# Sixty-four row scatters declared disjoint, and the expert weights moved in the POOL queue

## The chip, the cores and the metric

One core of one Trainium2 chip runs the whole program in one launch. The metric is the time of one execution in microseconds, taken on the device. Engines named here: PE (matrix multiply), DVE and ACT (elementwise), POOL (GpSimd, which also issues the indirect DMAs and the weight loads), SP (issues the plain DMAs).

## The reference

Linear attention with decay, then a mixture of experts with one expert per token.

- Attention: q, k, v are (4 batches, 8 heads, 768 positions, 64). Per head, with decay lam, each position gets the masked, decayed sum over its own block plus what a running 64x64 state `kv_state` of the blocks before it gives; the state is decayed and updated block by block. The result, heads side by side, is x of (3072 tokens, 512).
- Router: cosine logits of x against 8 expert embeddings, divided by tau; each token goes to its largest logit, with that softmax value as its gate.
- Experts: `out[mask] = gate * (relu(x[mask] @ w1[e]) @ w2[e])`, w1 of 512x1024 and w2 of 1024x512 for each of 8 experts, in float32 in memory.

## The kernel before, in words

The order of the instructions on every engine is the order in which they are written (a manual schedule); semaphores are put in by the framework from the tiles and DRAM tensors that instructions read and write.

**Attention** is a loop of 24 rounds of 128 tokens (6 rounds for each of 4 batches), software-pipelined: iteration i loads q, k, v of round i+3 (`load_round`, SP, a ring of 6 buffers each), transposes round i+2 on PE, makes the decayed keys `ks` of round i+2 on POOL (L242), does the output matmuls of round i, scales the state on POOL (`pool_kvt`, L295), and writes it with DVE (`ev_kv`, L307), which needs that POOL result. The first round of a batch has no state and is shorter. Iterations 0 to 7 also write zero rows into the scratch tensor (`zrow`, L470).

**Routing** goes by five groups of 6, 6, 6, 4 and 2 rounds. Once a group is done, DVE finds each token's expert and its row in the scratch `xs_dram` (one region of 3072 rows for each expert), and `scatter` (L428) sends each round's 128 rows (fp16 x, token number, gate) there with one indirect DMA issued by POOL: 24 in all. The list `todo` says at which iteration each comes; the scatters of the last two groups come after the loop's other work, the two of group 4 ahead of the four of group 3. The slot numbers `si` live in 2 buffers, used by groups in turn.

**Weights** come in 64 loads of a quarter matrix (`load_w`, L211 and L213), cast from float32 to fp16 by the DMA, issued by POOL: one in each iteration from i = 2 to 25, which brings experts 0 to 2, then eight behind each expert's scatters. `wpool` has 4 buffers for each of w1 and w2.

**Experts.** SP reads each expert's first 512 rows back (`load_xe`; expert 0 in four pieces), PE transposes them, then `pe_L1` and `pe_L2`. For each of 4 row blocks DVE scales the result into one of 6 `y_sb` buffers (L565) and POOL scatters the 128 rows to `out` (L567): 32 in all. Rows that hold no token carry an index out of bounds and are skipped. The read of expert e+4 reuses the buffer whose index column the last scatter of expert e reads. `pstart`, an iota on POOL (L516), stands between attention's last POOL work and the first of these scatters; DVE needs it (L584) before it scales the first result.

A block for experts with over 512 tokens follows the count; in this case's runs its loop bodies leave no instruction in the trace.

Of the kernel before, what the change touches and what calls it, by code (L numbers as in the profile page):

```python
# [9 lines left out]

# [11 lines left out]
def kernel(  # L22
# [19 lines left out]
    R = B * NBLK  # L42
    E, DM = moe_expert_emb.shape
# [4 lines left out]
    G = CAP // P  # L48
# [6 lines left out]
    groups = [list(range(0, 6)), list(range(6, 12)), list(range(12, 18)),  # L55
              list(range(18, 22)), list(range(22, 24))]
# [4 lines left out]

    const = ctx.enter_context(tc.tile_pool(name="const", bufs=1))
    dram = ctx.enter_context(tc.tile_pool(name="dram", bufs=1, space=bass.MemoryType.DRAM))
    wpool = ctx.enter_context(tc.tile_pool(name="wpool", bufs=4))
    xgp = ctx.enter_context(tc.tile_pool(name="xgp", bufs=3))
    rsm = ctx.enter_context(tc.tile_pool(name="rsm", bufs=2))

    xs_dram = dram.tile([E * ROWS, DM2], I32, name="xs_dram")

    w1_r = moe_w1.rearrange("e (c p) f -> e p c f", p=P)  # L70
    w2_r = moe_w2.rearrange("e (c p) d -> e p c d", p=P)
# [16 lines left out]
    def load_round(i):  # L88
        b, blk = divmod(i, NBLK)
        for src, store, nm in ((q, qn, "qn"), (k, kn, "kn"), (v, vn, "vn")):  # L90
            t = ring.tile([P, H, D], FP32, name=nm, tag=nm)
            nc.sync.dma_start(t, src[b, :, ds(blk * P, P), :].rearrange("h p d -> p h d"))
            store[i] = t
# [104 lines left out]
    wpos = [0]  # L198

    def load_w(n):  # L200
        for _ in range(n):
            if wpos[0] >= len(wq):
                return
            e, which, c = wq[wpos[0]]
            wpos[0] += 1
            if (e, 1) not in w_tiles:
                w_tiles[(e, 1)] = wpool.tile([P, DC, F], FP16, name="w1_sb", tag="w1")
                w_tiles[(e, 2)] = wpool.tile([P, FC, DM], FP16, name="w2_sb", tag="w2")
            t = w_tiles[(e, which)]
            if which == 1:  # L210
                nc.gpsimd.dma_start(t[:, c : c + 1, :], w1_r[e][:, c : c + 1, :])  # L211
            else:
                nc.gpsimd.dma_start(t[:, 2 * c : 2 * c + 2, :], w2_r[e][:, 2 * c : 2 * c + 2, :])  # L213

    def valid(i):
        return 0 <= i < R
# [15 lines left out]
    def ev_T(i):  # L232
        t = wk.tile([P, HP, P], FP32, name="qT", tag="qT", bufs=3)
        nc.vector.tensor_tensor(t, bank.pop(("q", i)), lamq, op=ALU.mult)
        qT[i] = t
        t = wk.tile([P, HP, P], FP32, name="kT", tag="kT")
        nc.scalar.copy(t, bank.pop(("k", i)))  # L237
        kT[i] = t
# [188 lines left out]

    def scatter(gi, j):  # L428
        nc.gpsimd.indirect_dma_start(  # L429
            out=xs_dram[:],  # L430
            out_offset=bass.IndirectOffsetOnAxis(ap=slot_i[gi][:, j : j + 1], axis=0),
            in_=xg[gi][:, j, :],
            in_offset=None,
        )
# [31 lines left out]
    for i in range(-2, R + 2):  # L466
        if i >= 0 and valid(i + LA):
            load_round(i + LA)
        if 0 <= i < E:
            nc.sync.dma_start(xs_dram[ds(i * ROWS, CAP), :].rearrange("(g p) d -> p g d", p=P),  # L470
                              zrow)
        if valid(i + 2):
            pe_T(i + 2)
            ev_T(i + 2)
            pool_ks(i + 2)
        if valid(i - 1):
            pe_X(i - 1)
            ev_X(i - 1)
        if valid(i - 2):
            pe_z(i - 2)  # L480
            ev_z(i - 2)
        run(i, "pe")
        if valid(i):
            pe_O(i)
            if i % NBLK < NBLK - 1:
                pe_kv(i)
                if i % NBLK > 0:
                    pool_kvt(i)
                ev_kv(i)
            ev_O(i)  # L490
        if valid(i - 1):
            pe_zT(i - 1)
            ev_zT(i - 1)
        run(i, "dve")
        if valid(i + 1):
            pe_ST(i + 1)
            ev_ST(i + 1)
        run(i, "pe2")
        run(i, "dve2")
        run(i, "pool")  # L500
        run(i, "pool2")
        if i >= 2:
            load_w(1)
    for key in sorted(todo):
        for fn, a in todo[key]:
            fn(*a)
    attn_ctx.close()


# [8 lines left out]
    with (  # L518
        tc.tile_pool(name="moe_x", bufs=4) as moe_x,
        tc.tile_pool(name="moe_sb", bufs=2) as moe_sb,  # L520
        tc.tile_pool(name="moe_y", bufs=6) as moe_y,
        tc.tile_pool(name="ps_mx", bufs=2, space=bass.MemoryType.PSUM) as ps_mx,
        tc.tile_pool(name="ps_h", bufs=3, space=bass.MemoryType.PSUM) as ps_h,
        tc.tile_pool(name="ps_y", bufs=3, space=bass.MemoryType.PSUM) as ps_y,
    ):
        xe, xTe, hT, idx = {}, {}, {}, {}

        def load_xe(e, split=1):
            t = moe_x.tile([P, G, DM2], I32, name="x_e", tag="x_e")
            src = xs_dram[ds(e * ROWS, CAP), :].rearrange("(g p) d -> p g d", p=P)  # L530
            for s in range(split):
                w = G // split
                nc.sync.dma_start(t[:, s * w : (s + 1) * w, :], src[:, s * w : (s + 1) * w, :])
            xe[e] = t

        def pe_xT(e):
            t = moe_sb.tile([P, DC, G, P], FP16, name="xTe", tag="xTe")
            for g in range(G):
                xtr = ps_mx.tile([P, DC, P], FP16, name="xtr", tag="xtr")
                for c in range(DC):  # L540
                    nc.tensor.transpose(xtr[:, c, :], xe[e][:, g, 0:DW].bitcast(FP16)[:, ds(P * c, P)], ident16)  # L541
                nc.scalar.copy(t[:, :, g, :], xtr)  # L542
            xTe[e] = t

        def pe_L1(e):
            t = moe_sb.tile([P, FC, CAP], FP16, name="hT", tag="hT")
            w = w_tiles[(e, 1)]
            for fc in range(FC):
                h_ps = ps_h.tile([P, CAP], FP32, name="h_ps", tag="h")
                for c in range(DC):  # L550
                    nc.tensor.matmul(h_ps, w[:, c, ds(P * fc, P)],  # L551
                                     xTe[e][:, c].rearrange("p g t -> p (g t)"),
                                     start=(c == 0), stop=(c == DC - 1))
                nc.scalar.activation(t[:, fc, :], h_ps, AF.Relu)  # L554
            hT[e] = t

        def pe_L2(e):
            w = w_tiles[(e, 2)]
            for g in range(G):
                y_ps = ps_y.tile([P, DM], FP32, name="y_ps", tag="y")  # L560
                for fc in range(FC):
                    nc.tensor.matmul(y_ps, hT[e][:, fc, ds(P * g, P)], w[:, fc, :],  # L562
                                     start=(fc == 0), stop=(fc == FC - 1))
                y = moe_y.tile([P, DM], FP32, name="y_sb", tag="y_sb")
                nc.vector.tensor_scalar(y, y_ps, xe[e][:, g, DW + 1 : DW + 2].bitcast(FP32),  # L565
                                        None, op0=ALU.mult)
                nc.gpsimd.indirect_dma_start(  # L567
                    out=out[:],
                    out_offset=bass.IndirectOffsetOnAxis(ap=xe[e][:, g, DW : DW + 1], axis=0),
                    in_=y[:],  # L570
                    in_offset=None,
                    bounds_check=N - 1,
                    oob_is_err=False,
                )

        load_xe(0, split=4)
        load_xe(1, split=2)
        load_xe(2)
        cnt_ps = ps_y.tile([P, DM], FP32, name="cnt_ps", tag="y")
        nc.tensor.matmul(cnt_ps[:, 0:E], ones16, ohcum, start=True, stop=True)  # L580
        nc.vector.tensor_scalar(last, cnt_ps[:, 0:E], -1.0, None, op0=ALU.add)
        nc.vector.tensor_reduce(mx, cnt_ps[:, 0:E], axis=AXL.X, op=ALU.max)

        nc.vector.tensor_tensor(  # L584
            below, cnt_ps[:, 0:E].unsqueeze(2).to_broadcast([P, E, R]),
            pstart.unsqueeze(1).to_broadcast([P, E, R]), op=ALU.is_gt)
        nc.vector.tensor_reduce(ntile_f, below, axis=AXL.X, op=ALU.add)
        nc.vector.tensor_scalar(ntile, ntile_f, float(G), None, op0=ALU.max)
        pe_xT(0)
        for e in range(E):  # L590
            pe_L1(e)
            if e + 1 < E:
                pe_xT(e + 1)
            if e + 3 < E:
                load_xe(e + 3)
            pe_L2(e)
            load_w(8)
# [5 lines left out]
    with tc.If(mreg > CAP, preferred_fallthrough_block=False):  # L603
        with (
# [5 lines left out]
            for e in range(E):  # L610
# [7 lines left out]
                with tc.For_i(G, end):  # L618
# [8 lines left out]
                        out=xo[:], out_offset=None, in_=xs_dram[:],  # L627
# [15 lines left out]
                    for fc in range(FC):  # L643
# [6 lines left out]
                        out=out[:],  # L650
# [37 lines left out]
```

## Time and profile before

| | |
|---|---|
| median of 3 runs | 392.25 us (389.97 to 394.6) |
| profiled execution | 393.91 us, of which the span from first to last instruction is 392.1 us |
[...]
| busy, of the span | PE 69%, PEld 47%, DVE 29%, ACT 31%, POOL 39% |
| DMA | 54.10 MB, mean 138 GB/s |
| weight loads | 64 of 256 KB, median 6.2 us from issue to landing |
| scatters to `xs_dram` | 24, 2.5 / 3.0 / 5.1 us to landing (min, median, max) |
| scatters to `out` | 32, 2.1 / 2.7 / 10.9 us to landing |
| DVE's scaling of one result (L565) | 751 ns, 32 of them |

Busy time is an average over an attention stage (to about 175 us), a handover (to 206 us), an expert stage (to 357 us) and a tail in which PE does nothing (to 392 us). No engine is near the full span, so the time is read from the waits of each stage. POOL's share counts the issue of its DMAs, not the time in which its queue stands behind a semaphore.

### The profile page before, as it was taken

To read this page: it belongs to the slowest core of one execution; us is meant where nothing else is said; L and a number is where in the kernel's file an instruction comes from. 1 tells how busy PE (TensorE), PEld (TensorE's weight loads), DVE (VectorE), ACT (ScalarE), POOL (GpSimd) and SP (SyncE) were. 2 spreads that over 40 slices of the span, in tenths; PEclk is the share of its full clock that TensorE was granted. 3 is DMA by queue.
4 is the path that set the end of the run, shared out by engine and by line. 5 is a ranking of instruction groups with operands and counts; after the bars stand their busy time and mean duration, and the time that the engine had idled before them with its cause. 6 is when DMAs were issued, how large, how long until landed. Compare 5 with 4: busy or idle time off the path is not lost. (4 is left out here: it accounts for less than half of the span.)

```text
span 392.1 us, 6263 instructions
## 1 busy us (share of the span) xinstructions
PE 269.1 (69%) x2426; PEld 184.6 (47%) x2426; DVE 114.8 (29%) x305; ACT 120.8 (31%) x257; POOL 152.4 (39%) x204
## 2 busy tenths in 40 slices
PE   0999897899069978930029999999979588492000
PEld 0899785899069967820014444444424134140000
DVE  2556446453157545641000302202101102012000
ACT  5244352344105442420014263362515042130000
POOL 2545162533474576263410252271532704322220
PEclk9999999899669998975557999999989979698555
DMA  9999999999969934243343139277393682921110
GB/s 164 238 251 242 242 239 216 198 213 206 228 120 184 176 72 70 41 94 67 67 129 117 43 77 214 91 145 157 88 211 103 126 178 65 183 96 38 55 75 2
DMA packets 100615, 54.10 MB, mean 138 GB/s; under 512 B 77782, under 2 KB 94166, under 8 KB 100576
## 3 DMA queue, kind: packets, MB, share of 16 engines
q0 software_dynamic: 17024, 26.25, 33.7%
q1 hardware_dynamic: 83552, 27.35, 31.7%
q8 instruction: 21, 0.34, 0.4%
q14 instruction: 18, 0.15, 0.1%
HBM read 56.68 MB, written 15.79 MB: 185 GB/s over the span
## 5 line engine op out<-in xcount | busy, mean ns | idle before, releaser
L567 POOL DMA_INDIRECT out_dram<-y_sb,x_e x32 | 32.0, 1001 | 125.9 <-issue 73.8
L551 PE MATMUL h_ps<-xTe,w_sb 128*128 128x512 f16 x256 | 65.5, 414 | 15.2 <-DMA w_sb<-in_moe_w_dram 14.4
L554 ACT ACTIVATE hT<-h_ps 128x512 f16<-128x512 f32 x64 | 38.2, 597 | 90.1 <-PE h_ps L551 90.1
L565 DVE TENSOR_SCALAR y_sb<-y_ps,x_e 128x512 f32<-128x512 f32 x32 | 24.0, 751 | 141.2 <-PE y_ps L562 70.1
L562 PE MATMUL y_ps<-w_sb,hT 128*128 128x512 f16 x256 | 56.7, 379 | 1.7 <-DVE y_sb L565 1.7
L551 PEld LDWEIGHTS <-w_sb 128*128 128x128 f16 x256 | 26.5, 105 | 53.2 <-DMA w_sb<-in_moe_w_dram 18.4
L429 POOL DMA_INDIRECT xs_dram<-xg,si x24 | 24.5, 1019 | 48.7 <-DMA xs_dram<-xg,si 35.3
L242 POOL TENSOR_TENSOR ks<-kn,kdec 128x512 f32<-128x512 f32 x24 | 25.0, 1046 | 38.5 <-DMA kn<-in_k_dram 21.2
L562 PEld LDWEIGHTS <-hT 128*128 128x128 f16 x256 | 24.7, 98 | 30.5 <-issue 2.0
L259 DVE TENSOR_TENSOR stm<-s_ps,mask 128x512 f32<-128x512 f32 x48 | 30.9, 686 | 15.6 <-PE s_ps L251 15.1
L541 PE MATMUL xtr<-ident,x_e 128*128 128x128 f16 x128 | 11.7, 229 | 26.4 <-DMA x_e<-xs_dram 20.3
L237 ACT COPY kT<-k_ps 128x512 f32<-128x512 f32 x24 | 14.1, 587 | 49.7 <-PE k_ps L227 46.1
L272 PE MATMUL o_ps<-stm,vn 128*64 128x128 f32 x384 | 28.6, 288 | 0.0
L251 PE MATMUL s_ps<-qT,kT 64*128 64x128 f32 x384 | 28.4, 288 | 0.0
L307 DVE TENSOR_TENSOR kv<-kv_ps,kvt 64x256 f32<-64x256 f32 x32 | 13.5, 422 | 48.6 <-PE kv_ps L283 26.4
L312 ACT COPY xT<-o_ps 128x512 f32<-128x512 f32 x24 | 14.1, 586 | 40.2 <-PE o_ps L272 40.2
L251 PEld LDWEIGHTS s_ps<-qT,kT 64*128 64x128 f32 x384 | 23.8, 191 | 4.2 <-issue 3.9
L542 ACT COPY xTe<-xtr 128x512 f16<-128x512 f16 x32 | 17.0, 589 | 24.8 <-DMA x_e<-xs_dram 24.6
L272 PEld LDWEIGHTS o_ps<-stm,vn 128*64 128x64 f32 x384 | 22.5, 143 | 3.7 <-issue 0.8
L213 POOL DMA_DIRECT2D w_sb<-in_moe_w_dram x32 | 23.7, 774 | 1.0 <-issue 1.0
L268 PE MATMUL o_ps<-qT,kv 128*128 128x128 f32 x160 | 24.1, 299 | 0.0
L295 POOL TENSOR_TENSOR kvt<-kv,lam 64x256 f32<-64x256 f32 x32 | 19.6, 613 | 9.8 <-DVE kv L307 6.6
(99 smaller groups left out, 309.2 us busy)
## 6 DMA issues: line engine op xcount, KB each, us to landing
w_sb<-in_moe_w_dram POOLq DMA_DIRECT2D x64, 256.0 KB, 6.2
qn<-in_q_dram SPq DMA_DIRECT2D x24, 256.0 KB, 7.2
kn<-in_k_dram SPq DMA_DIRECT2D x24, 256.0 KB, 4.6
vn<-in_v_dram SPq DMA_DIRECT2D x24, 256.0 KB, 5.1
xs_dram<-zrow SPq DMA_DIRECT2D x8, 516.0 KB, 7.9
x_e<-xs_dram SPq DMA_DIRECT2D x6, 516.0 KB, 10.2
x_e<-xs_dram SPq DMA_DIRECT2D x4, 129.0 KB, 2.0
x_e<-xs_dram SPq DMA_DIRECT2D x2, 258.0 KB
```

The costliest lines, as they stand in the source:

```text
L213: nc.gpsimd.dma_start(t[:, 2 * c : 2 * c + 2, :], w2_r[e][:, 2 * c : 2 * c + 2, :])
L242: nc.gpsimd.tensor_tensor(t, kn[i], kdec.unsqueeze(2).to_broadcast([P, H, D]), op=ALU.mult)
L251: nc.tensor.matmul(bank["s", h2, i][:, hp, :], kT[i][ds(64 * h2, 64), hp, :], qT[i][ds(64 * h2, 64), hp, :], start=(hp == 0), stop=True, s ...
L259: nc.vector.tensor_tensor(t[:, h2], bank.pop(("s", h2, i)), mask[:, h2], op=ALU.mult)
L268: nc.tensor.matmul(t[:, hp, :], kv2[i % 2][:, hp, :], qT[i][:, hp, :], start=(hp == 0), stop=False, skip_group_check=True)
L272: nc.tensor.matmul(t[ds(64 * h2, 64), hp, :], vn[i][:, 2 * hp + h2, :], stm[i][:, h2, hp, :], start=(blk == 0 and hp == 0), stop=True, ski ...
L429: nc.gpsimd.indirect_dma_start(out=xs_dram[:], out_offset=bass.IndirectOffsetOnAxis(ap=slot_i[gi][:, j : j + 1], axis=0), in_=xg[gi][:, j, :],
L551: nc.tensor.matmul(h_ps, w[:, c, ds(P * fc, P)], xTe[e][:, c].rearrange("p g t -> p (g t)"), start=(c == 0), stop=(c == DC - 1))
L554: nc.scalar.activation(t[:, fc, :], h_ps, AF.Relu)
L562: nc.tensor.matmul(y_ps, hT[e][:, fc, ds(P * g, P)], w[:, fc, :], start=(fc == 0), stop=(fc == FC - 1))
L565: nc.vector.tensor_scalar(y, y_ps, xe[e][:, g, DW + 1 : DW + 2].bitcast(FP32), None, op0=ALU.mult)
L567: nc.gpsimd.indirect_dma_start(out=out[:], out_offset=bass.IndirectOffsetOnAxis(ap=xe[e][:, g, DW : DW + 1], axis=0), in_=y[:], in_offset= ...
```

## The change

Both scatters get, each, a view of its own of the DRAM tensor, and the views are declared disjoint: the framework puts no wait between two of them. Accesses to the whole tensor (the zero rows, the reads of `load_xe`) still wait for all of them, and they for it. In the attention loop the loads run from i = 4 to 23 (20 instead of 24); 20 more follow in one burst behind the last scatter to the scratch, so that experts 0 to 4 have been asked for before the expert stage; `wpool` has 5 buffers. The eight loads behind each expert's scatters stay, and are expert 5's, 6's and 7's behind experts 0, 1 and 2.

```diff
+from concourse.ap import dram_disjoint_views
-    wpool = ctx.enter_context(tc.tile_pool(name="wpool", bufs=4))
+    wpool = ctx.enter_context(tc.tile_pool(name="wpool", bufs=5))
...
+    xs_views = dram_disjoint_views(xs_dram[:], R)
+    out_views = dram_disjoint_views(out, E * G)
...
     def scatter(gi, j):
         nc.gpsimd.indirect_dma_start(
-            out=xs_dram[:],
+            out=xs_views[groups[gi][j]],
...
-        if i >= 2:
+        if 4 <= i < R:
             load_w(1)
     for key in sorted(todo):
         for fn, a in todo[key]:
             fn(*a)
+    load_w(5 * 8 - wpos[0])
     attn_ctx.close()
...
                 nc.gpsimd.indirect_dma_start(
-                    out=out[:],
+                    out=out_views[e * G + g],
```

## Rows read from the trace of the kernel before

**Rows 1.** The chain of waits, near its end: start us, us, what.
```profile
379.23 2.61 DMA out_dram<-y_sb,x_e
```

**Rows 2.** Waits of the whole span: engine, line, waited for: total us, times, longest.
```profile
DVE y_sb L565 <- DMA out_dram<-y_sb,x_e: 52.1, 11, 13.8
...
POOL xs_dram L429 <- DMA xs_dram<-xg,si: 35.3, 17, 4.9
...
POOL out_dram L567 <- DMA w_sb<-in_moe_w_dram: 0.6, 2, 0.3
```

**Rows 3.** Timeline of ACT, attention: its copy of each round's output, one a round.
```profile
40.01 0.59 ACT L312 COPY xT<-o_ps 128x512 f32<-128x512 f32 x1 [0.82 <-PE o_ps L272]
45.49 0.59 ACT L312 COPY xT<-o_ps 128x512 f32<-128x512 f32 x1 [0.82 <-PE o_ps L272]
...
85.48 0.59 ACT L312 COPY xT<-o_ps 128x512 f32<-128x512 f32 x1 [0.82 <-PE o_ps L272]
89.61 0.59 ACT L312 COPY xT<-o_ps 128x512 f32<-128x512 f32 x1
...
115.10 0.59 ACT L312 COPY xT<-o_ps 128x512 f32<-128x512 f32 x1 [15.35 <-PE o_ps L272]
...
152.63 0.59 ACT L312 COPY xT<-o_ps 128x512 f32<-128x512 f32 x1 [6.66 <-PE o_ps L272]
```

**Rows 4.** Timeline of POOL, attention, the state's scaling behind scatters.
```profile
106.43 0.61 POOL L295 TENSOR_TENSOR kvt<-kv,lam 64x256 f32<-64x256 f32 x1 [2.06 <-DMA xs_dram<-xg,si]
```

**Rows 5.** Timeline of POOL, expert stage: start us, us, instruction [idle before <-releaser].
```profile
182.98 0.97 POOL L429 DMA_INDIRECT xs_dram<-xg,si  x1 [3.14 <-DVE mx L582]
...
198.25 0.97 POOL L429 DMA_INDIRECT xs_dram<-xg,si  x1 [1.74 <-DMA xs_dram<-xg,si]
...
248.29 1.02 POOL L567 DMA_INDIRECT out_dram<-y_sb,x_e  x1 [10.45 <-DMA out_dram<-y_sb,x_e]
...
382.61 0.98 POOL L567 DMA_INDIRECT out_dram<-y_sb,x_e  x1 [2.40 <-DMA out_dram<-y_sb,x_e]
```

**Rows 6.** Timeline of all engines, handover.
```profile
173.85 0.17 DVE L371 TENSOR_TENSOR oh<-ohr,ohm 128x16 f16<-128x16 f32 x1
...
177.48 0.75 POOL L374 TENSOR_TENSOR nrm<-nsq_all,half 128x2 f32<-128x2 f32 x1
...
181.98 0.17 DVE L403 CAST si<-sf 128x2 int32<-128x2 f32 x1 [2.64 <-DMA xs_dram<-xg,si]
```

**Rows 7.** Timeline of PE, expert stage.
```profile
206.21 8.96 PE L551 MATMUL h_ps<-xTe,w_sb 128*128 128x512 f16 x32 [0.77 <-ACT xTe L542]
...
217.04 7.07 PE L562 MATMUL y_ps<-w_sb,hT 128*128 128x512 f16 x32
...
232.89 7.07 PE L562 MATMUL y_ps<-w_sb,hT 128*128 128x512 f16 x32
...
354.81 1.89 PE L562 MATMUL y_ps<-w_sb,hT 128*128 128x512 f16 x8 [1.72 <-DVE y_sb L565]
```

**Rows 8.** Busy time by stretch: us, PE, PEld, DVE, ACT, POOL, PEclk, DMA share, GB/s.
```profile
206.00:287.00 81.00, 76.69 (x399) 36.58 (x400) 13.51 (x18) 34.07 (x61) 27.68 (x37) 0.97 0.53 118
```

**Rows 9.** Groups of the page: what | busy us, mean ns | idle before.
```profile
L242 POOL TENSOR_TENSOR ks<-kn,kdec 128x512 f32<-128x512 f32 x24 | 25.0, 1046 | 38.5 <-DMA kn<-in_k_dram 21.2
```

**Rows 10.** DMA queues, 80 to 103 us: packets, MB, share; issues: count, size, landing us.
```profile
q1 hardware_dynamic: 15468, 3.90, 80.6%
...
w_sb<-in_moe_w_dram POOLq DMA_DIRECT2D x3, 256.0 KB, 5.8
```

**Rows 11.** Weight loads, 330 to 348 us: ns min/median/max, first and last start us.
```profile
L211 POOL DMA_DIRECT2D w_sb<-in_moe_w_dram x4: 588/604/617, 330.8 to 332.5; - x4
L213 POOL DMA_DIRECT2D w_sb<-in_moe_w_dram x4: 784/802/808, 333.0 to 335.1; - x4
...
DMA to landing us min/median/max: 3.6/7.3/10.3
```

**Rows 12.** DMA issues, 231 to 249 us.
```profile
x_e<-xs_dram SPq DMA_DIRECT2D x1, 516.0 KB, 10.2
```

## The prediction

> **What bounds the kernel now.** I read the chain of waits first. It ends in scatters to `out` that wait for one another [rows 1]: POOL issues a scatter, its 128 rows land 2.6 us later, and only then may the next go. The table of waits shows the same thing at both places [rows 2]: POOL waited 35.3 us for earlier scatters to the scratch, and DVE 52.1 us in all for a scatter to give a `y_sb` buffer back. So the next step is to lay the stages side by side and see in each which wait ends last.
>
> *Attention.* ACT copies one round's output out of PSUM, so its copies are the clock of the loop. Undisturbed rounds are 45.49 - 40.01 = 5.48 us apart, and the short round of a batch 89.61 - 85.48 = 4.13 us [rows 3]. Two steps are much longer: before the copy at 115.10 ACT stood idle 15.35 us and before that at 152.63 6.66 us, against 0.82 us otherwise, so 14.5 + 5.8 = 20.3 us too much. Both are POOL's: the scaling of the state, which DVE and then PE need, is queued behind scatters that wait [rows 4]. A slower loss lies earlier. From 45.49 to 85.48 are six rounds, of which one short: 5 x 5.48 + 4.13 = 31.5 us, and they took 40.0. These 8.5 us are late loads of q, k and v.
>
> *Handover.* Six scatters leave between 182.98 and 198.25 [rows 5], and the first is late too: the slot numbers of the last group wait 2.64 us for a scatter that still reads their buffer, and `nrm`, on POOL, comes only at 177.48 though its inputs are older than `oh` at 173.85 [rows 6].
>
> *Experts.* From the second layer of one expert to that of the next it is 232.89 - 217.04 = 15.85 us with PE busy 76.69 of 81 us at a clock of 0.97 [rows 7, 8]. PE could keep that up, but falls back later, through full `y_sb` buffers and late weights. Behind each eight weight loads a scatter lands late and the next stands 10.45 us [rows 5]. PE ends at 354.81 + 1.89 = 356.7, and the last scatter starts only at 382.61: 25.9 us in which scatters are worked off.
>
> **The change, step by step.** The sum is made against the profiled execution, 393.91 us for a span of 392.1; it lies 1.7 us above the median of the runs.
>
> *Scratch scatters without waits, attention.* POOL then has per round at most `ks` (1.05), two halves of the state (0.61 each), two scatters (0.98 each) and a load (0.8): 5.0 us [rows 4, 5, 9, 11], under 5.48, so PE sets the pace. The 20.3 us go. What could be late next is the loads. In the 23 us from 80 to 103, with the DMA engines full, 3.90 MB of q, k and v moved, 4.96 rounds of 0.786 MB, so 4.64 us a round with 0.6 weight loads in each [rows 10]. A weight load costs 1.57 us where eight follow each other: the first landed at 330.8 + 3.6, the last at 335.1 + 10.3, 11.0 us for seven more [rows 11]. One load in each round makes 4.64 + 0.4 x 1.57 = 5.3 us, against PE's mean of 31.5 / 6 = 5.26. That is a tie; between 0 and 8 us of new lateness over twelve rounds I take 1.5, since the rows give the tie.
>
> *Two loads fewer at i = 2 and 3.* They leave the stretch in which loads are late: 2 x 1.57 = 3.1 us of the 8.5. The two at i = 24 and 25 lay beside other work: 0. Attention gains 20.3 + 3.1 - 1.5 = **21.9 us**.
>
> *Handover.* `nrm` runs at once and the slot numbers wait for nothing. After `oh` DVE has some 13 small operations at about 0.2 us, so the first scatter starts near 176.6 and the sixth five issues of 1.0 us later, at 181.6, against 198.25: **16.6 us**.
>
> *The burst of 20 loads.* It adds 20 issues of 0.6 to 0.8 us on POOL, and transfers that run beside the reads of `x_e`, which PE waits for. Before, matmuls began 206.21 - 198.25 = 8.0 us after the last scratch scatter. Beside eight weight loads a read of this size took 10.2 us [rows 12]. So it becomes 2.5 for the scatter's landing, 10.2, and 1.3 for the last transposes and copy: 14.0 us, **6.0 us lost**. The ends are 0 (the read is not disturbed) and 24 (it comes behind all 20 loads); the row is the nearest there is.
>
> [...]
>
> *New waits.* A scatter waited for a weight load issued eight DMAs before it [rows 2], so each POOL DMA waits for the eighth before it. The burst then holds POOL: the 20th goes out when the 12th has landed, 1 + 3.6 + 11 x 1.57 = 22 us after the last scratch scatter, about 27 with the reads of `x_e` beside them. Behind it stand `pstart`, for which DVE waits ahead of the first result, and expert 0's scatters. PE stops for DVE only at its third result, at 14.0 + 10.8 + 3.5 = 28.3 us. Cost 0, cover one microsecond; if the burst takes 5 us longer, it costs 5. Expert 0's first scatter lands behind the loads, near 43 us; the seventh result, which needs its buffer, is due at 46: cost 0 as well. Expert 5's loads end near 60 us and are needed at 96.
>
> *Experts.* From the first matmul: 10.8 us to the second layer (217.04 - 206.21, slow clock in it, as before), seven periods of 15.85, less 1.9 us of transposes that the last expert lacks, and 7.07 us: 126.9, against 356.7 - 206.2 = 150.5 us. **23.6 us**.
>
> *Tail.* The last scatter starts 1.2 us after PE's end (DVE's 0.75 and two hops) instead of 25.9: **24.7 us**. The 9.5 us behind it stay.
>
> Sum: 21.9 + 16.6 - 6.0 + 23.6 + 24.7 = 80.8 us, so 393.9 - 80.8 = **313 us**.
>
> **Rivals.**
>
> 1. *Equal turns.* [...] Chance 0.12.
>
> 2. *Transfers set the pace of attention.* If a load beside q, k and v costs twice the 1.57 us (it reads float32), a round takes 4.64 + 0.4 x 3.1 = 5.9 us, twelve rounds 8 us more: 321. For it speak the 8.5 us; against it that no round after 85.48 waited for loads. Chance 0.12.
>
> 3. *The burst goes first.* Expert 0's rows come behind 20 loads: 1 + 3.6 + 19 x 1.57 = 34.4, and 3.9 for the rest, 38 instead of 14 us: 337. Against it stands that a read got through beside eight loads at all. Chance 0.10.
>
> 4. *The waits stay*, under another name. Then only the bursts change: three instead of five stalls of about 11 us, the first scatter some 8 us later: near 380. Chance 0.05.
>
> 5. *Slower: the loads go one at a time.* Place: the counters that each POOL DMA shares with the eighth before it. If a load had to land before the next, 44 loads stand between the handover and expert 7. With the handover at 198.25 - 38.5 = 160 us and 20 us behind the last load, the time passes the old one at (392 - 180) / 44 = 4.8 us a load; at 5.0 the span would be 180 + 220 = 400 and the time 402. Single loads land in 3.6 us and more, so the price is near; but eight of them landed 1.57 us apart [rows 11]. Chance 0.04.
>
> **How the numbers follow.** The forecast of 313 has 0.55; 0.02 is left for no change. About 1% is what a measurement of this kernel tells from none. Faster 0.94, same 0.02, slower 0.04. The range reaches down to equal turns with the late loads gone (309.5 less 5.4, 304) and up over rival 2 and, by the burst's larger costs, nearly to rival 3: 303 to 335.
>
> **What would show it.** Right: no POOL wait named after a scatter; ACT's copies 5.5 us apart from round 11 on; the last scratch scatter near 160 us; PE's second layers 15.85 us apart to the end; the last scatter to `out` about 1 us behind PE. Wrong: PE waiting for `x_e` well over 14 us behind the last scratch scatter (rival 3), or for q and k (rival 2); DVE waiting for `pstart` while PSUM is full; `y_sb` waits among the first three experts.

## The result: 324.3 us, and the profile after

The changed kernel takes 324.27 us (median of 4 runs, 322.49 to 327.05) against 391.11 for the kernel before on the same chip: a ratio of 0.829 [0.820, 0.837]. The forecast of 313 us was 11 us too low, and the range of 303 to 335 holds the time. The profiled execution has a span of 325.2 us against 392.1, at a mean granted PE clock of 0.926 against 0.864. In the changed kernel's lines, attention stands 4 lower than before (L383 is now L387, L312 is L316) and the expert stage 5 lower (L562 is L567, L567 is L572).

Waits of the whole span after: engine, line, waited for: total us, times, longest.

```profile
POOL xs_dram L433 <- issue: 12.7, 23, 2.6
POOL w_sb L217 <- DMA w_sb<-in_moe_w_dram: 11.2, 7, 2.6
...
PE zb L387 <- DVE z_all L336: 9.9, 4, 4.0
...
PE y_ps L567 <- DVE below L589: 1.9, 1, 1.9
```

Both large rows of [rows 2] are gone: nothing waits for an earlier scatter to the scratch or for a `y_sb` buffer. What POOL now waits for in front of loads are loads (one load, at L217, stands 0.6 us for a scatter to `out`), and two waits of PE are left that matter below.

ACT's copy of each round's output after, which is the clock of attention, from round 12 (cf. [rows 3]):

```profile
86.29 0.58 ACT L316 COPY xT<-o_ps 128x512 f32<-128x512 f32 x1
91.78 0.59 ACT L316 COPY xT<-o_ps 128x512 f32<-128x512 f32 x1 [0.82 <-PE o_ps L276]
101.61 0.59 ACT L316 COPY xT<-o_ps 128x512 f32<-128x512 f32 x1 [5.18 <-PE o_ps L276]
...
128.56 0.59 ACT L316 COPY xT<-o_ps 128x512 f32<-128x512 f32 x1 [0.82 <-PE o_ps L276]
140.30 0.58 ACT L316 COPY xT<-o_ps 128x512 f32<-128x512 f32 x1 [7.09 <-PE o_ps L276]
...
155.82 0.58 ACT L316 COPY xT<-o_ps 128x512 f32<-128x512 f32 x1 [0.87 <-PE o_ps L276]
```

The two long steps are still there. The idle time of 15.35 us ahead of round 14 became 5.18, and the 6.66 ahead of round 20 did not shrink at all: 7.09.

POOL's timeline after, handover to end (cf. [rows 5]):

```profile
164.57 0.98 POOL L433 DMA_INDIRECT xs_dram<-xg,si  x1 [3.00 <-DVE mx L587]
165.85 0.97 POOL L433 DMA_INDIRECT xs_dram<-xg,si  x1 [0.30 <-issue]
...
170.94 0.96 POOL L433 DMA_INDIRECT xs_dram<-xg,si  x1 [0.30 <-issue]
171.90 2.96 POOL L217 DMA_DIRECT2D w_sb<-in_moe_w_dram  x4
...
181.23 0.70 POOL L217 DMA_DIRECT2D w_sb<-in_moe_w_dram  x1 [2.57 <-DMA w_sb<-in_moe_w_dram]
...
199.77 0.70 POOL L217 DMA_DIRECT2D w_sb<-in_moe_w_dram  x1 [1.24 <-DMA w_sb<-in_moe_w_dram]
200.48 0.18 POOL L521 IOTA pstart<- 128x24 f32 x1
...
314.69 0.98 POOL L572 DMA_INDIRECT out_dram<-y_sb,x_e  x1 [0.75 <-DVEq L608]
```

The six last scratch scatters are 1.27 us apart, the burst holds POOL until 200.5, and the last scatter to `out` follows PE's end by 1.07 us. PE's timeline after, expert stage (cf. [rows 7]):

```profile
184.71 9.02 PE L556 MATMUL h_ps<-xTe,w_sb 128*128 128x512 f16 x32 [0.77 <-ACT xTe L547]
...
195.60 3.62 PE L567 MATMUL y_ps<-w_sb,hT 128*128 128x512 f16 x16
201.10 3.61 PE L567 MATMUL y_ps<-w_sb,hT 128*128 128x512 f16 x16 [1.89 <-DVE below L589]
...
213.50 7.07 PE L567 MATMUL y_ps<-w_sb,hT 128*128 128x512 f16 x32
...
229.34 7.07 PE L567 MATMUL y_ps<-w_sb,hT 128*128 128x512 f16 x32
...
306.55 7.07 PE L567 MATMUL y_ps<-w_sb,hT 128*128 128x512 f16 x32
```

From 213.50 to 229.34 it is 15.84 us, as before, and the last of the eight second layers starts at 306.55. No wait of PE for weights or for a `y_sb` buffer stands between.

So the spans differ by 66.9 us, and this is where it comes from, to 0.1 us: attention (to the copy of round 23, 167.86 and 155.82) 12.0; from there to the last scratch scatter (30.4 and 15.1) 15.3; from that to the first expert matmul (7.96 and 13.77) -5.8; from that to PE's end (150.5 and 128.9) 21.6; from PE's end to the last scatter (25.91 and 1.07) 24.8; behind it (9.5 and 10.6) -1.1.

### The profile page after: what moved, and what is told of

It is laid out like the page before. It is cut to its first block, busy times and chain, and to the rows that moved or that the text cites. A ratio compares the mean times of both kernels' runs of the same rounds, so it can differ in the third digit from the quotient of the medians.

```text
span 325.2 us, 6259 instructions
## 1 busy us (share of the span) xinstructions
PE 261.9 (81%) x2426; PEld 183.7 (56%) x2426; DVE 120.2 (37%) x305; ACT 120.8 (37%) x257; POOL 151.7 (47%) x204
## 5 line engine op out<-in xcount | busy, mean ns | idle before, releaser
L572 POOL DMA_INDIRECT out_dram<-y_sb,x_e x32 | 31.9, 995 | 66.7 <-DVE y_sb L570 59.8
L556 PE MATMUL h_ps<-xTe,w_sb 128*128 128x512 f16 x256 | 58.5, 388 | 0.8 <-ACT xTe L547 0.8
L567 PE MATMUL y_ps<-w_sb,hT 128*128 128x512 f16 x256 | 56.7, 379 | 1.9 <-DVE below L589 1.9
L556 PEld LDWEIGHTS <-w_sb 128*128 128x128 f16 x256 | 25.4, 100 | 32.5 <-issue 2.6
L567 PEld LDWEIGHTS <-hT 128*128 128x128 f16 x256 | 24.8, 98 | 30.6 <-issue 2.2
L263 DVE TENSOR_TENSOR stm<-s_ps,mask 128x512 f32<-128x512 f32 x48 | 30.9, 685 | 16.2 <-PE s_ps L255 15.8
L433 POOL DMA_INDIRECT xs_dram<-xg,si x24 | 24.3, 1010 | 15.7 <-issue 12.7
L276 PE MATMUL o_ps<-stm,vn 128*64 128x128 f32 x384 | 29.7, 297 | 0.0
L217 POOL DMA_DIRECT2D w_sb<-in_moe_w_dram x32 | 23.4, 748 | 12.2 <-DMA w_sb<-in_moe_w_dram 11.2
L299 POOL TENSOR_TENSOR kvt<-kv,lam 64x256 f32<-64x256 f32 x32 | 19.5, 610 | 15.7 <-DVE kv L311 8.2
L316 ACT COPY xT<-o_ps 128x512 f32<-128x512 f32 x24 | 14.1, 586 | 32.2 <-PE o_ps L276 32.2
L546 PEld LDWEIGHTS <-x_e 128*128 128x128 f16 x128 | 8.8, 101 | 27.2 <-issue 22.9
```

The lines of the kernel that those rows point to most:

```text
L263: nc.vector.tensor_tensor(t[:, h2], bank.pop(("s", h2, i)), mask[:, h2], op=ALU.mult)
L276: nc.tensor.matmul(t[ds(64 * h2, 64), hp, :], vn[i][:, 2 * hp + h2, :], stm[i][:, h2, hp, :], start=(blk == 0 and hp == 0), stop=True, ski ...
L433: nc.gpsimd.indirect_dma_start(out=xs_views[groups[gi][j]], out_offset=bass.IndirectOffsetOnAxis(ap=slot_i[gi][:, j : j + 1], axis=0), in_ ...
L556: nc.tensor.matmul(h_ps, w[:, c, ds(P * fc, P)], xTe[e][:, c].rearrange("p g t -> p (g t)"), start=(c == 0), stop=(c == DC - 1))
L572: nc.gpsimd.indirect_dma_start(out=out_views[e * G + g], out_offset=bass.IndirectOffsetOnAxis(ap=xe[e][:, g, DW : DW + 1], axis=0), in_=y[ ...
```

## The experiments

The theory after the result: attention fell short because PE's rank step (`pe_rank`, L387, which counts tokens by expert once a group is done) stands in PE's queue ahead of a round's output matmuls. It needs the PSUM bank `zb`, which DVE gives back (`ev_z`, L336) only behind `rt_a` (six small operations that find each token's expert) and the round's masks. Rivals: loads pace attention; the burst is what cost the time; the run was a slow chip. All marks in us, from the profiled run of each:

| kernel | ratio to before | copy of round 23 | last scratch scatter, behind it | first matmul, behind that | PE stage | last scatter behind PE |
|---|---|---|---|---|---|---|
| before | 1 | 167.9 | 30.4 | 8.0 | 150.5 | 25.9 |
| after | 0.829 [0.820, 0.837] | 155.8 | 15.1 | 13.8 | 128.9 | 1.1 |
| e1 | 0.815 [0.810, 0.820] | 155.7 | 17.7 | 9.0 | 126.5 | 1.1 |
| e2 | 0.986 [0.981, 0.991] | 166.6 | 32.0 | 13.6 | 139.9 | 25.4 |
| e3 | 0.800 [0.797, 0.804] | 147.3 | 15.1 | 15.2 | 127.7 | 1.1 |
| e4 | 0.813 [0.810, 0.816] | 151.1 | 15.1 | 13.6 | 126.6 | 1.1 |
| e5 | 0.816 [0.811, 0.822] | 150.6 | 15.7 | 13.6 | 128.0 | 1.1 |
| e6 | 0.942 [0.936, 0.948] | 157.0 | 17.0 | 8.6 | 151.9 | 25.6 |
| e7 | 0.795 [0.791, 0.799] | 141.8 | 20.8 | 8.8 | 126.3 | 1.1 |
| e8 (after again) | 0.814 [0.809, 0.819] | 153.0 | 15.2 | 13.0 | 128.7 | 1.1 |
| e9 | 0.799 [0.794, 0.804] | 149.4 | 16.2 | 8.7 | 127.5 | 1.1 |
| e10 (e3 again) | 0.806 [0.799, 0.813] | 148.4 | 15.2 | 13.8 | 128.4 | 1.1 |

e1 to e4 ran on one chip, e5 to e8 on a second, e9 and e10 on a third; the kernel before took 395.9, 395.5 and 395.4 us there, so kernels are compared by ratio.

**e1, the views alone**: the weight loads and their four buffers as before.

```diff
-    wpool = ... bufs=5
+    wpool = ... bufs=4
-        if 4 <= i < R:
+        if i >= 2:
             load_w(1)
-    load_w(5 * 8 - wpos[0])
```

> Disjoint views as in the change, weight loads and their four buffers as before. Theory (the views carry the whole gain, the burst delays expert 0's rows): the last scratch scatter comes about 3 us later than in the changed kernel, because the two early loads are back, but matmuls of expert 0 begin 8 us behind it instead of 13.8, PE does not wait for pstart (1.9 us), and the loads behind each expert's scatters come in time for a period of 15.85 us: about 320 us, a little under the changed kernel's 324. Rival (the loads asked for early are needed): PE waits for weights at experts 3 to 7 as before, 14 us in all, and the time is 333 or more.

0.815: all of the gain. It is not told apart from the whole change run again (e8, 0.814, on another chip), nor from e4 on its own chip, which is the whole change but for the place of `pstart` (0.813). PE needs 126.5 us with four buffers and no burst, so the gain of the expert stage (24.0 us here, 23.6 forecast) is the views' alone. Without the burst the matmuls begin 9.0 us behind the last scratch scatter. The handover is 2.6 us longer: DVE's last slot numbers (`si`, L407) wait 1.70 us for a scatter that still reads their buffer, a wait that the changed kernel does not have, and a load stands among the last six scatters.

**e2, the loads alone**: both scatters write the whole tensors again.

```diff
-            out=xs_views[groups[gi][j]],
+            out=xs_dram[:],
-                    out=out_views[e * G + g],
+                    out=out[:],
```

> The burst, the five buffers and the loads of the change, scatters without views, so with their waits. Theory (scatter waits set attention's late rounds, the handover and the expert stage): attention about 3 us shorter, handover as before, and the chain of 32 scatters at 3.5 us each stays, with three stalls of 11 to 13 us behind loads instead of five, and its first scatter 18 us later: about 380 us. Rival (late weights were what held the expert stage): PE's 14.4 us of waits for weights and their slow clock go, and the time falls to 365 or less.

0.986, so 0.014 x 396 = 5.5 us: less than the 14 us or so of the expectation (380), and the rival's 365 is out. The expert stage wins 10.6 us, and 7.3 are lost between attention's end and the first matmul (5.6 of them behind the last scratch scatter); the tail stays at 25.4.

**e3, the rank step later**: the changed kernel with `pe_rank`, and `rt_b`, which reads it, behind the round's own work.

```diff
-            at(last + 1, "pe", pe_rank, gi)
-            at(last + 1, "dve", rt_b, gi)
+            at(last + 1, "pe2", pe_rank, gi)
+            at(last + 1, "dve2", rt_b, gi)
```

> The changed kernel, with pe_rank and rt_b of the first four groups moved behind the next round's pe_ST and ev_ST in the same iteration. Theory (the long rounds that are left, at i = 8, 14 and 20, come from the rank matmuls standing ahead of that round's output matmuls on PE, where they wait for DVE's ev_z, which stands behind rt_a and the mask multiplication; 4 us of idle PE each, and 2 us more at the lower clock): the excess of 4.5 + 5.3 + 6.8 us in these steps falls to under 2 us each, and the time to 311 to 316 us. Rival (these rounds wait for loads of q, k, v or for POOL): the copies of ACT stay 9.5 to 11.7 us apart there, and the time stays at 324 us.

The wait `PE zb <- DVE z_all` has no row any more, and the copies of rounds 13, 14, 19 and 20 in e3 are:

```profile
92.15 0.59 ACT L316 COPY xT<-o_ps 128x512 f32<-128x512 f32 x1 [0.82 <-PE o_ps L276]
98.37 0.59 ACT L316 COPY xT<-o_ps 128x512 f32<-128x512 f32 x1 [1.56 <-PE o_ps L276]
...
125.07 0.59 ACT L316 COPY xT<-o_ps 128x512 f32<-128x512 f32 x1 [0.82 <-PE o_ps L276]
132.07 0.59 ACT L316 COPY xT<-o_ps 128x512 f32<-128x512 f32 x1 [2.34 <-PE o_ps L276]
```

The steps of 9.83 and 11.74 us became 6.22 and 7.00. From round 13 to 23 attention takes 55.2 us; on the same chip it takes 61.6 in e1 and 61.3 in e4, and 64.0 in the changed kernel's profile on another. Round 8's step fell too, from 9.48 to 6.22, but round 9's then rose from 6.01 to 10.00, with a wait of PE for a key block (L231, 1.6 us). In the time the kernel is at 0.800 where e1 and e4 on its chip are at 0.815 and 0.813, with intervals that do not meet: about 0.013 x 396 = 5 us. The median of 316.7 us is just above the 311 to 316 expected.

**e4, `pstart` ahead of the burst.**

```diff
+    pstart = const.tile(...); nc.gpsimd.iota(pstart, ...)
     load_w(5 * 8 - wpos[0])
-    pstart = const.tile(...); nc.gpsimd.iota(pstart, ...)
```

> The changed kernel, with the iota pstart ahead of the burst of 20 loads on POOL. Theory (DVE stands at below until POOL has issued the burst, and PE at its third result for that): the 1.9 us wait of PE goes, and the median falls by 1.5 to 2.5 us, to about 322. Rival (expert 0's first scatter, or something else behind the burst, keeps the same end): no change, 324 us.

PE's wait for `below` is gone, and the stage takes 126.6 us instead of 128.9 and 128.7 (e8). The time, 0.813, is e8's, on another chip: 2 us are no more than attention differs from run to run.

**e5, POOL quiet beside `rt_a`**: no load in the iterations in which `rt_a` stands (7, 13 and 19), and one scatter fewer there.

```diff
-                at(last + 3 + j * 4 // len(tl), "pool", scatter, gi, j)
+                at(last + 3 + j * 3 // len(tl), "pool", scatter, gi, j)
-        if 4 <= i < R:
-            load_w(1)
+        if 4 <= i < R and i % 6 != 1:
+            load_w(2 if i % 6 == 2 else 1)
```

> The changed kernel, with POOL kept free of DMAs while DVE does rt_a: no weight load in iterations 7, 13 and 19 (two in the next), and the six scatters of a group in three iterations, two each, instead of four, so that none is left in 13 and 19. Theory (POOL's work lengthens single operations of rt_a from 0.2 to between 0.4 and 1.4 us, and PE's rank matmuls wait behind them): the operations beside no POOL work go back to 0.2 us, and the steps at rounds 14 and 20 become 1 to 2 us shorter each than in the changed kernel run beside it, 2 to 4 us in all. Rival (the order of DVE's work alone makes the wait): the steps keep their 9.8 and 11.7 us, and the time does not change.

0.816, no gain over e8. The longest wait of PE at L387 fell from 3.9 to 2.9 us, and the step of round 20 from 11.38 to 8.82; that of round 14 rose from 8.24 to 9.42. Inconclusive: what POOL beside `rt_a` costs is not settled by it.

**e6, the scratch views alone**: e1 with the scatters to `out` as before.

```diff
-                    out=out_views[e * G + g],
+                    out=out[:],
```

> Views for the scatters to the scratch alone; those to the output wait as before, and loads and buffers are as before. Theory (the two sets of waits cost in different stages and add up): attention and handover as with all views, last scratch scatter near 172 us instead of 198, the expert stage and tail as before, 186 us from there: 0.93 to 0.94 of the time before. Rival (time gained ahead of the experts is given back, since the scatters to the output set the end): within 2% of the time before.

0.942, at the upper end of the 0.93 to 0.94 expected. Waits of e6, of the same form as above:

```profile
DVE y_sb L569 <- DMA out_dram<-y_sb,x_e: 71.3, 14, 14.8
```

The stage (151.9) and the tail (25.6) are those of before, and attention and handover those of e1. e6 less e1, 0.127 x 396 = 50 us, is the worth of the views of `out` (the two ran on two chips); the prediction's two terms for it make 48.3.

**e7, e3's edits with late loads, four buffers and no burst**: attention's 24 loads go from i = 10 on, one in each iteration and from i = 18 two.

```diff
-        if 4 <= i < R:
-            load_w(1)
+        if i >= 10:
+            load_w(1 if i < 18 else 2)
-    load_w(5 * 8 - wpos[0])
```

> All views, pe_rank and rt_b later as in e3, four weight buffers, no burst: 24 loads in attention, one in each iteration from 10 to 17 and two from 18 to 25, and eight behind each expert's scatters as before. Theory (early loads delay q, k and v; the burst delays expert 0's rows by 5 us and pstart; the loads behind the scatters come in time): late loads of q, k, v cost 2 to 4 us instead of 5.6, matmuls begin 8 to 9 us behind the last scratch scatter, PE never waits for weights: 0.77 to 0.785 of the time before, 302 to 308 us where before takes 392. Rival (loads in pairs beside the last scatters slow POOL and DVE, or experts 3 to 7 come late): 0.80, no better than e3.

0.795, at the rival's end. Attention ends at 141.8 and the matmuls begin 8.8 us behind the last scratch scatter, but the handover grew from 15.1 to 20.8 us. POOL's timeline in e7:

```profile
146.05 1.54 POOL L217 DMA_DIRECT2D w_sb<-in_moe_w_dram  x2
147.57 0.78 POOL L378 TENSOR_TENSOR nrm<-nsq_all,half 128x2 f32<-128x2 f32 x1
148.55 1.08 POOL L433 DMA_INDIRECT xs_dram<-xg,si  x1 [0.20 <-issue]
154.59 1.00 POOL L433 DMA_INDIRECT xs_dram<-xg,si  x1 [4.96 <-DVE mx L586]
```

and of DVE:

```profile
153.57 0.17 DVE L407 CAST si<-sf 128x2 int32<-128x2 f32 x1 [3.90 <-DMA xs_dram<-xg,si]
```

`nrm` stands behind a pair of loads, the last slot numbers wait 3.90 us for a scatter that still reads their buffer (the scatter at 148.55 was issued behind that pair), and another pair stands among the last six scatters. The wait for `si` stands wherever loads go on to i = 25 (2.64 us before; 1.70, 1.4 and 3.90 in e1, e6 and e7), and in no kernel with views whose loads end earlier.

**e8, the changed kernel again** on the chip of e5 to e7.

> The changed kernel once more, on the chip of these runs, as the measure for e5. Every theory: 0.82 to 0.835 of the time before, and steps of 9 to 12 us at rounds 8, 14 and 20 again, though the length of single operations of rt_a beside POOL work may differ from run to run.

0.814 against 0.829: the same kernel, with intervals that just miss each other, and below the 0.82 to 0.835 expected. Of the steps of 9 to 12 us expected at rounds 8, 14 and 20, only the last came (7.46, 8.24 and 11.38). Attention ended 2.8 us earlier; differences of this size between chips are not read as effects here.

**e9, the loads clear of the last scatters** (the diff is against e7): e7 with one load in each iteration from 8 to 13 and two from 14 to 20, and twelve behind expert 0's scatters. **e10** is e3 again beside it.

```diff
-        if i >= 10:
-            load_w(1 if i < 18 else 2)
+        if 8 <= i < 21:
+            load_w(1 if i < 14 else 2)
-            load_w(8)
+            load_w(12 if e == 0 else 8)
```

> As the kernel with the late loads and the rank later, but all 20 loads are asked for inside attention by step 20 (from step 8 on, one a step up to 13 and two from 14 to 20), so that none stands beside the last scatters; no burst, four buffers. My theory (pairs of loads on POOL beside the last scratch scatters cost that kernel 5.7 us of handover): xT(23) copied near 142, the last scratch scatter 15 us behind it, matmuls 8.5 us after that, 126.4 of stage, span near 303, and 0.77 to 0.785 of before. Rival (the loads cost the same wherever they stand, or pairs in the middle of attention hold POOL's gathers and scatters): 0.795, no better than the kernel it is made from; then a wait of ACT or DVE for POOL stands in steps 14 to 20.

> The kernel with five buffers, the burst and the rank later, run again beside the one with loads inside attention. 0.80 of before as it was, with matmuls 13.5 to 15.3 us behind the last scratch scatter. Theory of the loads: it is slower than the other by 8 to 12 us, 5 of them between the last scratch scatter and the first matmul. Rival: within 3 us of it.

e9's 0.799 is the rival's. The handover came back to 16.2 us without the wait for `si`, as the theory of e7 said, but attention paid it: rounds 14 and 19 took 7.76 and 8.65 us. PE's timeline in e9:

```profile
118.57 0.66 PE L225 MATMUL q_ps<-ident,qn 128*128 128x128 f32 x4
121.43 1.03 PE L231 MATMUL k_ps<-ident,kn 128*128 128x128 f32 x4 [2.20 <-DMA kn<-in_k_dram]
```

A key block came late. Two loads a round went there; with one a round, no wait for q, k or v stood in the changed kernel after 95 us. That the second load made the block late is likely, not shown. e10 is at 0.806, behind e9 by 0.007, some 3 us, with intervals that overlap: the rival's, and not the 8 to 12 us of the theory. Its matmuls begin 13.8 us behind the last scratch scatter against 8.7, the 5 us expected, but its attention and handover are 1.9 us shorter. e7 is the fastest kernel run, about 7 us ahead of the changed kernel on its chip (0.795 and 0.814), and not told apart from e9.

## Why the prediction came out as it did, point by point

**Attention: 21.9 us forecast, 12.0 measured, the step that failed.** The step says "The 20.3 us go. What could be late next is the loads." For the two early loads' 3.1 us, round 13 is copied 3.3 earlier (91.78 instead of 95.09; 89.1 to 90.9 in e4, e5 and e8, so part of the match is luck). After that no wait for a load of q, k or v stood, where I took 1.5. But of the 20.3 us, the idle of 14.5 fell to 5.18 - 0.82 = 4.4, and that of 5.8 became 7.09 - 0.82 = 6.3: 9.7 us came. The steps behind these two, of rounds 15 and 21, lost 1.1 (6.38 and 6.01 instead of 5.62 and 5.62). More work stood behind the scatters at the same two rounds, and it was in the trace of before. PE's timeline in the kernel before:

```profile
98.28 0.27 PE L328 MATMUL zb<-ident,zT 128*128 128x128 f32 x1
111.17 0.20 PE L383 MATMUL zb<-oh,ltri 128*128 128x48 f16 x1 [12.62 <-DVE z_all L332]
...
148.69 0.20 PE L383 MATMUL zb<-oh,ltri 128*128 128x48 f16 x1 [3.92 <-DVE z_all L332]
```

I read ACT's idle time, saw POOL's scaling behind a scatter [rows 4], and put the whole of it to that. PE, the engine that ACT waits for, stood at the rank step both times, and DVE's timeline of before shows the two parts of that wait at round 20:

```profile
143.90 0.42 DVE L307 TENSOR_TENSOR kv<-kv_ps,kvt 64x256 f32<-64x256 f32 x1 [3.93 <-POOL kvt L295]
...
145.05 0.20 DVE L361 TENSOR_REDUCE zmax<-z_all 128x6 f32<-128x48 f32 x1
...
148.47 0.16 DVE L332 TENSOR_TENSOR z_all<-z_all,zb 128x8 f32<-128x8 f32 x1
```

DVE stood 3.93 us for POOL; that part went. From 145.05 to 148.63 it needed 3.6 us of its own work before the bank came back; that part needs no scatter, and it stayed. In the changed kernel PE still stands at the rank step:

```profile
131.74 0.27 PE L332 MATMUL zb<-ident,zT 128*128 128x128 f32 x1
136.02 0.20 PE L387 MATMUL zb<-oh,ltri 128*128 128x48 f16 x1 [4.01 <-DVE z_all L336]
...
136.24 2.06 PE L272 MATMUL o_ps<-qT,kv 128*128 128x128 f32 x8
138.22 1.98 PE L276 MATMUL o_ps<-stm,vn 128*64 128x128 f32 x16
```

and DVE's timeline after shows what it waits for:

```profile
129.94 0.20 DVE L365 TENSOR_REDUCE zmax<-z_all 128x6 f32<-128x48 f32 x1
130.18 0.90 DVE L367 TENSOR_TENSOR dz<-z_all,zmax 128x48 f32<-128x48 f32 x1
131.11 1.41 DVE L370 TENSOR_SCALAR ohr<-dz 128x48 f32<-128x48 f32 x1
132.56 0.55 DVE L371 TENSOR_TENSOR ohr<-ohr,rev 128x48 f32<-128x48 f32 x1
...
133.81 1.29 DVE L263 TENSOR_TENSOR stm<-s_ps,mask 128x512 f32<-128x512 f32 x2
135.02 0.68 DVE L238 TENSOR_TENSOR qT<-q_ps,lamq 128x512 f32<-128x512 f32 x1
...
135.81 0.16 DVE L336 TENSOR_TENSOR z_all<-z_all,zb 128x8 f32<-128x8 f32 x1
```

Six routing operations, the masks and the queries stand in DVE's queue ahead of the operation that gives the bank back. The same work that took 3.6 us before takes 6.0 here, from 129.94 to 135.97, since the six took 3.84 instead of 1.40 (see the last section); so nothing of round 20's idle time was gained. Of the 6.3 us too much in round 20, 4.0 are this wait and about 1.9 the slow matmuls behind it (2.06 + 1.98 against 1.06 + 1.09 in an undisturbed round). e3 shows the cause: with the rank step behind the output matmuls, about 6 of the 61 us from the copy of round 13 to that of round 23 go on its chip, and attention ends at 147.3, near the 167.9 - 21.9 = 146.0 of the forecast (148.4 in e10).

**Handover: 16.6 forecast, 15.3 measured.** The first scatter leaves 8.75 us behind the last copy, `nrm` and the slot numbers wait for no scatter. The scatters go 1.27 us apart and not 1.0, since 0.30 us lie between two issues: 5 x 0.27 = 1.35 us. The views alone do not bring all of this: e1, with loads at i = 24 and 25, has 17.7 us here instead of 15.1, so those two loads, which I put at 0, were worth 2.6 us.

**Burst beside `x_e`: -6.0 forecast, -5.8 measured.** Four kernels without the burst (e1, e6, e7, e9) begin 8.6 to 9.0 us behind the last scratch scatter, those with it 13.0 to 15.2. The sum of 2.5 + 10.2 + 1.3 us had the right terms: the last scatter lands after 2.5 us, the four pieces of the read take 9.6 from the first issue (173.71) to the last landing (183.29), and PE begins 1.4 behind that. The 10.2 was taken from one read of 516 KB and not from four pieces issued over 1.4 us, so that the sizes agree is partly luck. The pieces after, with the median time to landing:

```profile
x_e<-xs_dram SPq DMA_DIRECT2D x4, 129.0 KB, 7.4
```

The second took 6.6 us from its issue, the fourth 8.2. The lower end of the range rests on equal turns (rival 1), with a read of 6.7 us: a term that no run shows. In its place the runs showed a whole read of 9.6 us, and four loads of the burst landed in that time (176.19 to 183.09). So the rival is out.

**New waits: 0 forecast, 1.9 measured.** The place was right and the cover too short: the 20th load left POOL at 200.47, 29.5 us behind the last scratch scatter and not 27, so PE stood 1.89 us at its third result. Each of the last eleven loads of the burst left about 0.3 us behind the landing of the load issued eight before it (the 20th at 199.77, the 12th landed at 199.5). e4 takes the wait of PE away. No other wait came: expert 0's scatters landed by 211.4 without a `y_sb` wait.

**Experts and tail: 23.6 and 24.7 forecast, 21.6 and 24.8 measured.** The stage takes 128.9 us, which is the forecast's 126.9 and the 1.9 us just named; e1, e4 and e7 have 126.3 to 126.6. The tail is 1.07 us (forecast 1.2). Behind the last scatter it is 10.6 us instead of 9.5; nothing shown says why.

**Rivals.** Rival 1 is answered above. Rival 2's time of 321 is near the result, and its mechanism is not what happened: what is missing from the forecast was lost at rounds 14 and 20, and no wait for q or k stood there. At two loads a round, in e9, one wait for a key block stood (2.20 us). Rival 3 (the burst first) is out, since the first matmul comes 13.8 us behind the last scratch scatter and not 38; so is rival 5 (one load at a time): from the tenth on, the loads of the burst went 1.7 to 3.3 us apart. Rival 4 is out: no scatter waits for a scatter any more. The theory that this chip or run took longer explains a part of the miss: the same kernel took 0.814 of before in e8, which would be 318 us here, so about half of the 11 us differs between chips or runs. The rest is about what e3 takes away (0.800, which would be 313). And half of the change does nothing that can be measured: views alone are at 0.815, the whole at 0.814 to 0.829. The burst's 5 us and PE's 1.9 us pay away what the moved loads win (round 13 comes 2 to 4 us earlier than in e1, and the handover is 2.6 shorter), and weights were in time with four buffers once scatters no longer held POOL (PE waits for them 14.4 us in the kernel before, and not in e1).

## What to carry to other kernels

When an idle time is to be removed, read at that same moment every engine in the chain, not only the first culprit: what stands second in an in-order queue (here a PSUM bank handed back behind six small DVE operations, 4.01 us of PE) can take over when the first is gone. Put a step that few wait for behind the round's own work in a queue that all wait for. And test the halves of a change one at a time: here one half held all of the gain that can be measured.

## What the runs showed of the hardware

**The wait of PE at round 20 cost twice.** Two stretches of the changed kernel, one of undisturbed rounds and one behind the wait at round 20: us, PE, PEld, DVE, ACT, POOL, PEclk, DMA share, GB/s.

```profile
112.00:117.40 5.40, 5.40 (x79) 4.99 (x78) 3.59 (x10) 2.42 (x7) 4.11 (x5) 1.00 1.12 222
136.20:141.40 5.20, 5.20 (x55) 4.82 (x52) 0.23 (x1) 0.58 (x1) 0.19 (x1) 0.55 0.08 15
```

Behind the wait of 4.01 us the granted clock is 0.55, where it is 1.00 in the undisturbed stretch; the eight matmuls of L272 take 2.06 us instead of 1.06. Behind the wait of 3.24 us ahead of round 14 they took 1.14, and the next group 1.80 instead of 1.09.

**Small DVE operations took longer beside some of POOL's work.** The six operations of `rt_a` took 1.40 us in the kernel before (107.53 to 108.93, each 0.19 to 0.21) and 3.84 in the changed one (129.94 to 133.78), with the same sizes. POOL's timeline after, same stretch:

```profile
129.53 1.07 POOL L433 DMA_INDIRECT xs_dram<-xg,si  x1 [0.21 <-issue]
130.59 0.80 POOL L217 DMA_DIRECT2D w_sb<-in_moe_w_dram  x1
131.40 1.07 POOL L246 TENSOR_TENSOR ks<-kn,kdec 128x512 f32<-128x512 f32 x1
```

The operation at 131.11 ends at 132.52, when `ks` ends (132.47), and the one at 130.18, 0.90 us long, ends at 131.08 in the middle of a load's issue. This recurs: the operations of `rt_a` that were running when a scatter's issue passed into a load's took 1.05 us ahead of round 14 in the changed kernel (from 93.90) and 1.08 ahead of round 20 in e3 (from 126.94), and ended about 0.5 us into the load's. But not all of POOL's work went with it. POOL's timeline in the kernel before:

```profile
107.12 1.36 POOL L374 TENSOR_TENSOR nrm<-nsq_all,half 128x6 f32<-128x6 f32 x1
```

Four operations of `rt_a` ran within this one at 0.19 to 0.21 us each. The operation that ended with `ks` had begun 0.29 us ahead of it. e5, with POOL quieter there, had one stretched operation of 0.86 us at round 20 instead of four (0.90, 1.41, 0.55 and 0.40), and no better time; whether an instruction of POOL's holds DVE, which, and by what, stays open.
